# Rebuilding 64-bit weights with one pass on ScalarE instead of VectorE, and moving the softmax sums' chain one step

## The chip, the cores and the metric

The kernel runs on one core of a Trainium2 chip. Its time is device microseconds (us) of one execution; a median over runs is given. TensorE does the matmuls, VectorE and ScalarE the element work, GpSimd (POOL in the profile) the rest of it, and SyncE issues most of the DMAs. In the profile TensorE is PE (PEld is its weight load), VectorE is DVE, ScalarE is ACT and SyncE is SP.

## What is computed

Two batches of a three-stage block, in float32:

```
attention:  8 heads, 768 positions, head size 64
            scores = q k^T / 8; kept where key < n_sink (4) or 0 <= query - key < window (128)
            a = softmax(scores);  x = a v                        -> x: 2 x 768 x 512
MLP:        h = relu(x w_in)                      w_in 512 x 1024, given as 64-bit floats
            gate = sigmoid(conv over 3 positions of h)           conv_w 3 x 1024, 64-bit
            y = (h * gate) w_out                  w_out 1024 x 512, given as 64-bit floats
experts:    4 causal attention experts of size 64 on y, softmax, wo, weighted top-2 sum
```

## The kernel before

**Stages as steps.** The work is written out by hand as steps. `run_phases` (line 46) takes phases, each a start, a count and a list of stages with a lag, and emits at every step, in the order of the string `ORD1` (line 78), whatever stage is due then. Each engine runs its instructions in exactly that order. Attention of batch 0 (`a0`) takes steps 0 to 23: step i works on query tile qt = i // 4 (128 queries) and head pair pr = i % 4. Attention of batch 1 (`a1`) starts at step 24, the MLP (`m`) at step 30, the experts when both are through.

**Attention of batch 0 from qt = 2 on** (steps 8 to 23) is "overlaid" (`a1_S_overlaid`, line 506): TensorE writes the scores against the query tile's own keys into one PSUM bank (`own`) and those against the previous key tile into another (`old`); VectorE copies the old ones over the upper triangle of the own ones (line 518) and takes the maximum (line 519); ScalarE scales it (line 520) and takes the two exponentials with their sums (line 522). Every second step TensorE transposes four such tiles (line 571), ScalarE copies them out (line 574 through the helper at line 532), and GpSimd splits them with two selects (lines 575 and 577). GpSimd also copies the sink columns together (line 613).

**The sums' chain.** Once per query tile, after its last head pair, `attn_phase` (line 681) emits with a lag in steps taken from `LAGS[0]` (line 74): r (sum plus epsilon and reciprocal on VectorE, lines 527 and 528), rT (transpose on TensorE, line 545, copy, and a DMA store to DRAM, line 549), rB (two DMA loads that spread it over the partitions, line 556), xm (product with the attention output, line 560, VectorE, which frees the output's PSUM bank), xh (rounded copy, ScalarE, line 532), xl (the remainder, VectorE, line 670) and halo (small GpSimd copies). The order inside a step that matters here is: the weight background's first half (`more`), xl, S, sL, V, sV, xm, rT, sT, T, TT, the background's tail and second half (`misc`), r, xh.

**The weights.** Sixteen blocks of 128 x 512 64-bit numbers are loaded (line 379, two raw buffers; the load of block i+2 is issued after the last pass over block i) and each made into two float32r parts. `f64_fast` (line 334) makes the float from the upper word w1 and the lower word w0: mag (ScalarE, line 346, magnitude of w1, with an accumulated check), expo (VectorE, line 350, shift left by 3), top (VectorE, line 353, sign of w1), low (VectorE, line 356, three bits of w0). Then hi (line 538 or 540: ScalarE, VectorE or GpSimd by the letters of `WHI`) and lo (line 420, VectorE). mag of the next block is emitted together with low of this one.

**Their pace** is a budget of nominal nanoseconds (`background`, line 447): 550 a step in steps 4 to 23, 650 in 24 to 29, 1200 from step 30, each in two halves. A pass is emitted when its nominal cost (the list in `weight_steps`: 480 for expo, 860 for top, 860 for low) is in the budget. hi and lo are not in it: one of them is taken per step (`tail_step`), two from step 30.

The PSUM banks (8) are handed out to all of this by `psB` (line 117).

Of the kernel before, what the change touches and what calls it, by code (L numbers as in the profile page):

```python
# [12 lines left out]
U32 = mybir.dt.uint32  # L13
I64 = mybir.dt.int64
AF = mybir.ActivationFunctionType
ALU = mybir.AluOpType
# [8 lines left out]
KW = P + 2  # L25
# [14 lines left out]
F64_LO = 2.0**-15  # L40
F64_HI = 122879.9921875
GUARD = 2.0**-96
BIG = 3.0e38


# [25 lines left out]
BG0 = 550  # L71
BG1 = 650
BG2 = 1200
LAGS = ((1, 2, 1, 6, 4, 5, 6, 5, 2, 8, 8, 10, 11), (1, 1, 2, 6, 3, 4, 5, 3, 2, 5, 6, 7, 7))
LAGM = (1, 2, 3)
A2_N = 2
EVT = 'aaadadada'
# [11 lines left out]
class Kernel:  # L89
# [93 lines left out]
    def narrow(self):  # L183

        nc = self.nc
        g, ok = self.sm(1, "g"), self.guard
        nc.vector.tensor_scalar(ok, ok, GUARD, None, op0=ALU.is_lt)
        nc.vector.tensor_reduce(g, ok, axis=AX.X, op=ALU.add)
# [4 lines left out]
    def indices(self):  # L193
# [5 lines left out]
        nc.gpsimd.iota(self.kix, pattern=[[1, 2 * P]], base=0, channel_multiplier=0)  # L199
        nc.vector.tensor_scalar(z, rel[:, P:], 0.0, BIG, op0=ALU.is_lt, op1=ALU.mult)  # L200
        nc.vector.tensor_tensor(self.relx[:, P:], rel[:, P:], z, op=ALU.add)
# [132 lines left out]
    def f64_fast(self, raw, n, slot):  # L334

        nc = self.nc
        w = raw.bitcast(I32).rearrange("p (n two) -> p n two", two=2)  # L340
        w0, w1 = w[:, :, 0], w[:, :, 1]
        st = {}

        def mag():
            st["u"] = self.Wt([P, n], I32, "f64u")
            nc.scalar.activation(st["u"].bitcast(F32), w1.bitcast(F32), AF.Abs, scale=2.0**-111,
                                 accum_out=self.guard[:, slot : slot + 1])

        def expo():
            nc.vector.tensor_scalar(st["u"], st["u"], 3, None, op0=ALU.logical_shift_left)  # L350

        def top():
            nc.vector.scalar_tensor_tensor(st["u"], w1, -0x80000000, st["u"], op0=ALU.bitwise_and, op1=ALU.bitwise_or)

        def low():
            nc.vector.scalar_tensor_tensor(st["u"], w0, 29, st["u"], op0=ALU.logical_shift_right, op1=ALU.bitwise_or)
            st["c"] = st["u"].bitcast(F32)

        return st, [(0, mag), (480, expo), (860, top), (860, low)]

    def weight_steps(self):


        nc = self.nc
        order = []
        for f0 in range(0, NF, NF // 2):
            for f in range(f0, f0 + NF // 2 + 4):
                if f < f0 + NF // 2:
                    order.append((self.w_in, f, self.win))
                if f >= f0 + 4:  # L370
                    order.append((self.w_out, f - 4, self.wout))
        n = len(order)
        raws = {}

        def load(i):
            if i < n:
                src, f, _ = order[i]
                raws[i] = self.pRaw.tile([P, DM], I64, tag="raw", bufs=2, name=self.nm("raw"))
                nc.sync.dma_start(raws[i], src[f])

        boxes = [{} for _ in range(n)]

        def ahead(i):

            boxes[i]["st"], boxes[i]["ops"] = self.f64_fast(raws.pop(i), DM, i)
            boxes[i]["ops"][0][1]()

        steps = []
        if self.halves:
            steps.append((0, lambda: ahead(0)))  # L390
        for i in range(n):
            box = boxes[i]

            def step(i, k, box):
                if k == 0 and not self.halves:
                    box["st"], box["ops"] = self.f64_ops(raws.pop(i), DM)
                if k or not self.halves:
                    box["ops"][k][1]()
                if k == 3:
                    load(i + 2)  # L400
                    if self.halves and i + 1 < n:
                        ahead(i + 1)
                    self.tails.append([lambda: hi(i, box), lambda: lo(i, box)])

            steps += [(c, lambda i=i, k=k, box=box: step(i, k, box)) for k, c in enumerate((0, 480, 860, 860) if self.halves else (670, 335, 600, 600))]

        def part(i):
            _, f, dst = order[i]
            return [w[:, f].rearrange("p a c -> p (a c)") for w in dst]

        def hi(i, box):
            if self.halves:
                self.scaled(WHI[i], part(i)[0], box["st"]["c"], 2.0**-8)
            else:
                self.copy(WHI[i], part(i)[0], box["st"]["c"])

        def lo(i, box):
            h, l = part(i)
            if self.halves:
                nc.vector.scalar_tensor_tensor(l, box["st"]["c"], 2.0**-8, h.bitcast(F32), op0=ALU.mult, op1=ALU.subtract)  # L420
            else:
                nc.gpsimd.tensor_tensor(l, box["st"]["c"], h.bitcast(F32), op=ALU.subtract)
            self.ready.add((order[i][2][0].name, order[i][1]))

        return steps, lambda: (load(0), load(1))
# [30 lines left out]
    def a1_S(self, b, qt, pr):  # L456
# [39 lines left out]
        for j in range(2):  # L496
            nc.vector.tensor_tensor_reduce(out=Pt[:, j, :N], in0=ps[j][:, :N], in1=mask, scale=-SCALE,  # L497
                                           scalar=BIG, op0=ALU.add, op1=ALU.min, accum_out=nmx[:, j : j + 1])
        for j in range(2):
# [6 lines left out]
    def a1_S_overlaid(self, t, qt, pr, ps, Pt, nmx, sums):  # L506


        nc = self.nc
        w = KW + 2  # L510
        own, old = (x[:, : 2 * n].rearrange("p (j c) -> p j c", j=2) for x, n in zip(ps, (w, KW)))
        o = 2 * (qt % 2)
        for dst, kt in ((own[:, :, o : o + KW], qt), (old, qt - 1)):
            for j in range(2):
                nc.tensor.matmul(dst[:, j], t["q", qt][:, pr, j, :], t["k"][:, kt, pr, :], start=(j == 0), stop=(j == 1),
                                 skip_group_check=True)
        take = self.causal[:, 3 * P - o : 3 * P - o + KW].bitcast(I32)
        nc.vector.copy_predicated(own[:, :, 2 - o : 2 - o + KW], take[:, None, :].to_broadcast([P, 2, KW]), old)
        nc.vector.tensor_reduce(nmx, own, axis=AX.X, op=ALU.max, negate=True)
        nc.scalar.mul(nmx, nmx, SCALE)  # L520
        for j in range(2):
            nc.scalar.activation(Pt[:, j, :w], own[:, j], AF.Exp, bias=nmx[:, j : j + 1], scale=SCALE,
                                 accum_out=sums[:, j : j + 1])
# [225 lines left out]
    def attn_general(self, pool):  # L749
        nc = self.nc  # L750
        for b in range(B):
# [6 lines left out]
            for qt in range(NT):  # L758
# [10 lines left out]
                for h in range(H):  # L769
# [3 lines left out]
                    for c0, c1 in ((0, 4), (4, NT)):  # L773
# [5 lines left out]
                    nc.vector.tensor_tensor(pp, ps[:, :S], keep, op=ALU.mult)  # L779
                    nc.vector.tensor_tensor_reduce(out=pp, in0=pp, in1=pen, scale=-SCALE, scalar=BIG,  # L780
                                                   op0=ALU.add, op1=ALU.min, accum_out=nmx)
# [268 lines left out]
    def a2_S(self, b, qt, p, j):  # L1050
# [12 lines left out]
        for i, (lo, hi) in enumerate(pieces):  # L1063
# [6 lines left out]
            else:  # L1070
                nc.vector.tensor_tensor_reduce(out=Pt[:, lo:hi], in0=ps[:, : hi - lo], in1=self.causal[:, 4 * P + lo - hi : 4 * P], scale=-1.0,  # L1071
                                               scalar=BIG, op0=ALU.add, op1=ALU.min, accum_out=nm[:, i : i + 1])
        if len(pieces) == 2:
# [106 lines left out]
    def program(self, general):  # L1180
# [5 lines left out]
        with ExitStack() as ctx:  # L1186
# [34 lines left out]
            else:  # L1221
# [18 lines left out]
                self.fixed()  # L1240
                first = [self.attn_phase(b, b * NSTEP, LAGS[b], self.attn_misc(b)) for b in range(B)]
                m1 = NSTEP + MLP_START
# [109 lines left out]
```

## Time and profile before

| | |
|---|---|
| median of 3 runs | 380.1 us (378.39 to 380.71) |
| the profiled execution | 378.69 us |
| its span, first to last instruction | 377.0 us |
| TensorE clock granted | 0.996 |
| busy: PE / DVE / ACT / POOL | 359.7 / 275.9 / 259.9 / 132.0 us |

The profiled execution's span leaves 1.7 us of its time outside; the execution itself is 0.4% under the median. "Busy" of an engine is the time in which at least one of its instructions ran; where one instruction takes longer than its like, all of its duration counts. TensorE instructions overlap, and the modelled tail of a matmul can cover a short gap.

### The profile page before, as it was taken

What the parts mean: (1) busy time and instruction counts of PE and PEld (TensorE: products, weight loads), DVE (VectorE), ACT (ScalarE), POOL (GpSimd) and SP (SyncE); (2) the same over time, 40 slices, a digit from 0 to 9 for tenths busy, and PEclk for the clock granted to TensorE, in tenths of its full rate; (3) what the DMA queues carried; (4) which work ended last, traced back from release to release, by engine and by line L of the source; (5) the groups of instructions that cost most, each with busy time, mean ns of one, the idle gap of its engine ahead of it and who ended that gap; (6) DMA issues with size and microseconds to landing.
All of it is one profiled execution on the core that took longest, in us unless ns stands there. A gap on an engine that the chain in (4) does not pass through costs nothing.

```text
span 377.0 us, 8947 instructions
## 1 busy us (share of the span) xinstructions
PE 359.7 (95%) x3198; PEld 333.8 (89%) x3198; DVE 275.9 (73%) x800; ACT 259.9 (69%) x786; POOL 132.0 (35%) x254
## 2 busy tenths in 40 slices
PE   8898879999999999999999999999999999999994
PEld 5677767879899999999999999999999899978984
DVE  5589989889987997877865757237779697578631
ACT  4877768776876876635755875339878698859841
POOL 8016554244343333563521322310024134406310
PEclk9999999999999999999999999999999999999998
DMA  7953656433442301000111010000000010101112
GB/s 179 350 147 113 192 177 212 153 112 115 149 132 86 113 0 58 3 28 24 44 42 44 22 57 2 0 2 2 2 2 0 3 39 26 52 2 57 57 39 83
DMA packets 21844, 27.51 MB, mean 73 GB/s; under 512 B 2112, under 2 KB 14496, under 8 KB 21792
## 3 DMA queue, kind: packets, MB, share of 16 engines
q1 hardware_dynamic: 20560, 26.21, 21.9%
q10 hardware_dynamic: 1232, 0.66, 0.8%
q8 instruction: 27, 0.44, 0.5%
q14 instruction: 25, 0.20, 0.2%
HBM read 23.66 MB, written 3.19 MB: 71 GB/s over the span
## 4 chain that ended last, share of the span: by engine, by line
PE 65%; DVE 10%; ACT 6%; issue 2%; POOL 1%; DMA 1%; ACTq 0%; DVEq 0%
PE psB L854 15%; PE psB L810 14%; PE psB L1004 9%; PE psB L1128 5%; PE psB L932 5%; PE psB L1104 4%; PE psB L1152 3%; PE psB L640 2%; PE psB L1067 2%; PE psB L1066 2%; PE psB L483 2%; PE psB L598 1%; ACT P L1077 1%; ACT P L500 1%; DVE P L497 1%
## 5 line engine op out<-in xcount | busy, mean ns | idle before, releaser
L854 PE MATMUL psB<-g,wouthf 128*128 128x256 f32 x384 | 70.4, 281 | 0.3 <-POOL g L839 0.2
L854 PEld LDWEIGHTS psB<-g,wouthf 128*128 128x128 f32 x384 | 58.9, 188 | 0.7 <-POOL g L839 0.5
L1092 POOL TENSOR_SCALAR P<-P,r 128x256 f32<-128x256 f32 (+5 forms) x48 | 30.2, 643 | 82.5 <-DVE r L1090 45.6
L810 PE MATMUL psB<-xh,winhf 128*128 128x258 f32 x192 | 56.6, 295 | 0.0
L810 PE MATMUL psB<-xl,winhf 128*128 128x258 f32 x192 | 54.3, 283 | 0.0
L810 PE MATMUL psB<-xh,winlf 128*128 128x258 f32 x192 | 54.2, 282 | 0.0
L854 PE MATMUL psB<-g,woutlf 128*128 128x256 f32 x192 | 53.8, 280 | 0.0
L839 POOL TENSOR_TENSOR g<-ht,g 128x256 fp32r<-128x256 f32 x48 | 33.6, 701 | 52.9 <-ACT g L833 46.2
L826 ACT ACTIVATE ht<-ht 128x256 f32<-128x256 f32 x48 | 20.1, 419 | 27.9 <-DVE ht L824 27.8
L500 ACT ACTIVATE P<-P,nm 128x260 f32<-128x260 f32 (+2 forms) x64 | 30.5, 479 | 10.4 <-DVE nm L497 10.2
L831 DVE SCALAR_TENSOR_TENSOR ht<-ht 128x256 f32<-128x256 f32 x48 | 23.8, 496 | 18.7 <-ACT ht L826 18.7
L810 PEld LDWEIGHTS psB<-xh,winhf 128*128 128x128 f32 x192 | 36.4, 189 | 0.3 <-ACT ht L813 0.2
L810 PEld LDWEIGHTS psB<-xl,winhf 128*128 128x128 f32 x192 | 36.5, 190 | 0.0
L810 PEld LDWEIGHTS psB<-xh,winlf 128*128 128x128 f32 x192 | 36.3, 189 | 0.0
L854 PEld LDWEIGHTS psB<-g,woutlf 128*128 128x128 f32 x192 | 36.2, 188 | 0.0
L817 POOL TENSOR_SCALAR ht<-ht,cw 128x256 f32<-128x256 f32 x24 | 15.5, 648 | 56.9 <-ACT ht L813 51.4
L1077 ACT ACTIVATE P<-P,nm 128x256 f32<-128x256 f32 (+3 forms) x48 | 26.8, 561 | 4.7 <-DVE nm L1071 4.6
L824 DVE SCALAR_TENSOR_TENSOR ht<-ht,cw 128x256 f32<-128x256 f32 x48 | 27.7, 577 | 1.7
L1004 PE MATMUL psB<-yh,wqh 128*128 128x256 f32 x96 | 27.2, 283 | 0.0
L1004 PE MATMUL psB<-yl,wqh 128*128 128x256 f32 x96 | 27.0, 281 | 0.0
L1004 PE MATMUL psB<-yh,wql 128*128 128x256 f32 x96 | 26.9, 280 | 0.0
L1071 DVE CUSTOM_DVE_ANT_0 P<-psB,causal 128x256 f32<-128x256 f32 (+3 forms) x48 | 22.6, 485 | 5.8 <-PE psB L1067 5.4
(190 smaller groups left out, 1010.2 us busy)
## 6 DMA issues: line engine op xcount, KB each, us to landing
raw<-in_w_in_dram SPq DMA_DIRECT2D x8, 512.0 KB, 4.2
raw<-in_w_out_dram SPq DMA_DIRECT2D x8, 512.0 KB, 3.2
v<-in_v_dram SPq DMA_DIRECT2D x12, 256.0 KB, 5.2
R<-rD SPq DMA_DIRECT2D x24, 128.0 KB, 2.9
out_dram<-ot SPq DMA_DIRECT2D x11, 256.0 KB, 2.0
k<-in_k_dram SPq DMA_DIRECT2D x8, 260.0 KB, 3.9
raw<-in_wqkv_dram SPq DMA_DIRECT2D x8, 193.0 KB, 2.4
q<-in_q_dram SPq DMA_DIRECT2D x6, 256.0 KB, 3.2
```

Of the source, the lines that this page charges most:

```text
L500: nc.scalar.activation(Pt[:, j, :N], Pt[:, j, :N], AF.Exp, bias=nmx[:, j : j + 1], scale=-1.0, accum_out=sums[:, j : j + 1])
L810: nc.tensor.matmul(ps[:, :XW], w[:, f, kc, :], x[:, kc, :], start=(i == 0), stop=(i == len(ops) - 1))
L824: nc.vector.scalar_tensor_tensor(t1, h[:, 2 : 2 + CH], self.cw[:, 2 * NF + f : 2 * NF + f + 1], t1, op0=ALU.mult, op1=ALU.add)
L826: nc.scalar.activation(t1, t1, AF.Tanh)
L831: nc.vector.scalar_tensor_tensor(t1, t1, 1.0, h[:, 1 : 1 + CH], op0=ALU.add, op1=ALU.mult)
L839: eng.tensor_tensor(g[:, 1], t1, g[:, 0].bitcast(F32), op=ALU.subtract)
L854: nc.tensor.matmul(self.m1y[d // 2][:, d % 2, :], w[:, f, d, :], g[:, k], start=(first and i == 0 and d % 2 == 0), stop=(last and i == 2), ...
L932: nc.tensor.matmul(ps[:, :NVG], y[:, kc, ts_], w[:, kc, c0 : c0 + NVG], start=(i == 0), stop=(i == len(ops) - 1))
L1004: nc.tensor.matmul(ps, w[:, kc, c0 : c0 + P], y[:, kc, :], start=(i == 0), stop=(i == len(ops) - 1))
L1071: nc.vector.tensor_tensor_reduce(out=Pt[:, lo:hi], in0=ps[:, : hi - lo], in1=self.causal[:, 4 * P + lo - hi : 4 * P], scale=-1.0, scalar=B ...
L1077: nc.scalar.activation(Pt[:, lo:hi], src, AF.Exp, bias=nm[:, 0:1], scale=sg, accum_out=sums[:, j, i : i + 1])
L1092: nc.gpsimd.tensor_scalar(Ps[j][:, :N], Ps[j][:, :N], r[:, j : j + 1], 1.0, op0=ALU.mult, op1=ALU.mult)
```

## The change

Four edits. ScalarE gets one more pass per weight block (w0, read as an unsigned integer, is scaled and written back in place as its three upper bits); VectorE's three passes become two (shift u and join w0; then join the sign), and the third, `expo`, does nothing. The nominal cost of `expo` falls from 480 to 0. In `LAGS[0]` the entries r, rB, rT, xm, xh, xl and halo grow by one step. In the overlaid scores `old` takes the first bank and is computed first, `own` the second.

```diff
+LOW3 = (2.0**-29 * (1 - 2.0**-16), 7.5 * 2.0**-16 - 0.5)
...
-LAGS = ((1, 2, 1, 6, 4, 5, 6, 5, 2, 8, 8, 10, 11), (1, 1, 2, 6, 3, 4, 5, 3, 2, 5, 6, 7, 7))
+LAGS = ((2, 2, 1, 6, 4, 5, 6, 6, 3, 9, 9, 11, 12), (1, 1, 2, 6, 3, 4, 5, 3, 2, 5, 6, 7, 7))
...
             nc.scalar.activation(st["u"].bitcast(F32), w1.bitcast(F32), AF.Abs, scale=2.0**-111,
                                  accum_out=self.guard[:, slot : slot + 1])
+            nc.scalar.activation(w0, w0.bitcast(U32), AF.Copy, scale=LOW3[0], bias=LOW3[1])
 
         def expo():
-            nc.vector.tensor_scalar(st["u"], st["u"], 3, None, op0=ALU.logical_shift_left)
+            pass
 
         def top():
+            nc.vector.scalar_tensor_tensor(st["u"], st["u"], 3, w0, op0=ALU.logical_shift_left, op1=ALU.bitwise_or)
+
+        def low():
             nc.vector.scalar_tensor_tensor(st["u"], w1, -0x80000000, st["u"], op0=ALU.bitwise_and, op1=ALU.bitwise_or)
-
-        def low():
-            nc.vector.scalar_tensor_tensor(st["u"], w0, 29, st["u"], op0=ALU.logical_shift_right, op1=ALU.bitwise_or)
             st["c"] = st["u"].bitcast(F32)
 
-        return st, [(0, mag), (480, expo), (860, top), (860, low)]
+        return st, [(0, mag), (0, expo), (860, top), (860, low)]
...
-            steps += [(c, ...) for k, c in enumerate((0, 480, 860, 860) if self.halves else (670, 335, 600, 600))]
+            steps += [(c, ...) for k, c in enumerate((0, 0, 860, 860) if self.halves else (670, 335, 600, 600))]
...
-        own, old = (x[:, : 2 * n].rearrange("p (j c) -> p j c", j=2) for x, n in zip(ps, (w, KW)))
+        old, own = (x[:, : 2 * n].rearrange("p (j c) -> p j c", j=2) for x, n in zip(ps, (KW, w)))
-        for dst, kt in ((own[:, :, o : o + KW], qt), (old, qt - 1)):
+        for dst, kt in ((old, qt - 1), (own[:, :, o : o + KW], qt)):
```

## Rows read from the trace of the kernel before

**Rows 1.** The page's first part: busy time, share and instructions of each engine.
```profile
PE 359.7 (95%) x3198; PEld 333.8 (89%) x3198; DVE 275.9 (73%) x800; ACT 259.9 (69%) x786; POOL 132.0 (35%) x254
```

**Rows 2.** Windows: stretch, its length, busy us of each engine, granted clock, DMA.
```profile
18.67:54.45 35.78, 30.55 (x301) 26.71 (x303) 32.54 (x69) 25.50 (x105) 17.42 (x40) 1.00 0.51 159
65.00:111.00 46.00, 44.52 (x418) 40.30 (x418) 40.83 (x109) 33.60 (x101) 17.62 (x34) 1.00 0.40 130
```

**Rows 3.** Waits of PE, whole span: who for whom, us in total, times, longest.
```profile
PE psB L545 <- DVE su L528: 3.7, 5, 1.0
...
PE psB L515 <- DVE psB L518: 0.7, 1, 0.7
PE psB L640 <- ACT PT L532: 0.6, 1, 0.6
```

**Rows 4.** Timeline of DVE: start, duration, line; in brackets the idle time before.
```profile
43.07 0.42 DVE L518 COPY_PREDICATED psB<-causal,psB 128x260 f32<-128x260 int32 x1
43.53 0.43 DVE L519 TENSOR_REDUCE nm<-psB 128x2 f32<-128x264 f32 x1
43.88 0.68 DVE L560 TENSOR_TENSOR R<-psB,R 128x512 f32<-128x512 f32 x1
44.48 0.42 DVE L518 COPY_PREDICATED psB<-causal,psB 128x260 f32<-128x260 int32 x1
...
45.72 0.69 DVE L356 SCALAR_TENSOR_TENSOR f64u<-raw,f64u 128x512 int32<-128x512 int32 x1
46.33 0.61 DVE L527 TENSOR_SCALAR su<-su 128x8 f32<-128x8 f32 x1
46.97 0.20 DVE L528 RECIPROCAL su<-su 128x8 f32<-128x8 f32 x1
47.09 1.07 DVE L670 TENSOR_TENSOR xl<-R,xh 128x512 fp32r<-128x512 f32 x1
...
49.01 0.42 DVE L350 TENSOR_SCALAR f64u<-f64u 128x512 int32<-128x512 int32 x1
49.34 0.43 DVE L518 COPY_PREDICATED psB<-causal,psB 128x260 f32<-128x260 int32 x1
...
51.40 0.69 DVE L420 SCALAR_TENSOR_TENSOR winlf<-f64u,winhf 128x512 fp32r<-128x512 f32 x1 [0.85 <-ACT winhf L538]
52.01 1.12 DVE L353 SCALAR_TENSOR_TENSOR f64u<-raw,f64u 128x512 int32<-128x512 int32 x1
```

**Rows 5.** Timeline of POOL beside them.
```profile
45.76 1.15 POOL L575 TENSOR_SCALAR_AFFINE_SELECT PT<-PT 128x512 f32<-128x512 f32 x1 [1.58 <-ACT PT L532]
46.98 0.64 POOL L577 TENSOR_SCALAR_AFFINE_SELECT PT<-PT 128x512 f32<-128x512 f32 x1
...
51.61 0.98 POOL L577 TENSOR_SCALAR_AFFINE_SELECT PT<-PT 128x512 f32<-128x512 f32 x1
```

**Rows 6.** One source line each: durations min/median/max ns, first and last start.
```profile
L346 ACT ACTIVATE f64u<-raw x16: 653/670/698, 13.1 to 133.1; 128x512 f32<-128x512 f32 x16
...
L350 DVE TENSOR_SCALAR f64u<-f64u x17: 178/427/976, 10.8 to 137.0; 128x512 int32<-128x512 int32 x16, 128x24 int32<-128x24 int32 x1
...
L353 DVE SCALAR_TENSOR_TENSOR f64u<-raw,f64u x16: 673/684/1123, 15.0 to 140.3; 128x512 int32<-128x512 int32 x16
```

**Rows 7.** Timeline of ACT: mag, and the next maximum's scaling.
```profile
47.10 0.68 ACT L346 ACTIVATE f64u<-raw 128x512 f32<-128x512 f32 x1
...
49.12 0.20 ACT L520 ACTIVATE nm<-nm 128x2 f32<-128x2 f32 x1 [1.25 <-DVE nm L519]
```

**Rows 8.** Timeline of DVE, early MLP.
```profile
71.39 0.98 DVE L350 TENSOR_SCALAR f64u<-f64u 128x512 int32<-128x512 int32 x1 [1.54 <-ACT f64u L346]
```

**Rows 9.** Timeline of PE, early MLP.
```profile
76.60 0.71 PE L483 MATMUL psB<-k,q 64*128 64x130 f32 x6 [0.34 <-ACT PT L532]
77.81 0.27 PE L545 MATMUL psB<-ident,su 128*8 128x128 f32 x1 [0.50 <-DVE su L528]
```

**Rows 10.** DMA issues: KB each, us from issue to landing.
```profile
raw<-in_w_in_dram SPq DMA_DIRECT2D x8, 512.0 KB, 4.2
```

More of the change, by code (lines that the diff above doesn't have):

```diff
@@ L403, in step @@
                     self.tails.append([lambda: hi(i, box), lambda: lo(i, box)])
-            steps += [(c, lambda i=i, k=k, box=box: step(i, k, box)) for k, c in enumerate((0, 480, 860, 860) if self.halves else (670, 335, 600, 600))]
+            steps += [(c, lambda i=i, k=k, box=box: step(i, k, box)) for k, c in enumerate((0, 0, 860, 860) if self.halves else (670, 335, 600, 600))]
         def part(i):
```

## Prediction, made before the changed kernel ran

> **What bounds the kernel now.** I read the busy shares first, then windows, then the waits of TensorE, then the VectorE timeline. TensorE is busy for 359.7 of 377.0 us [rows 1], so most of the kernel can't become shorter by freeing another engine. The windows show where it can: in the 16 overlaid steps, 18.67 to 54.45 us, TensorE shows 30.55 of 35.78 us, VectorE 32.54, ScalarE 25.50 [rows 2]. TensorE's figure there is flattered: its waits in this stretch are mostly for the sums' reciprocal, 3.7 us in five waits over the whole span [rows 3]. The VectorE timeline shows passes nearly end to end, and its idle time is little, 35.78 - 32.54 = 3.2 us; the largest piece is 0.85 us for a rounded weight from ScalarE [rows 4]. So VectorE sets the pace of the overlaid steps, and each microsecond off its queue there is a microsecond off the end, as long as nothing else takes its place. In the early MLP, 65 to 111 us, TensorE has 44.52 of 46.00 [rows 2]: at most 1.5 us of visible idle is to be had. After 111 us VectorE doesn't hold TensorE up, and I cost the change there at nothing.
>
> Two things make VectorE's passes long. One is the work: from start to next start a weight pass takes 0.60 us (45.72 to 46.33), the shift of `expo` 0.33 (49.01 to 49.34), the product xm 0.60 (43.88 to 44.48), a score pair 0.81 (43.07 to 43.88) [rows 4]. The other is stretching: the 128 x 8 addition of r takes 0.61 us, the reciprocal of the same size behind it 0.20; xl takes 1.07 where the like passes take 0.68; `top` 1.12 where its median is 0.684 [rows 4, 6]. Each coincides with a GpSimd select: r ends just as the select of 45.76 to 46.91 does, xl overlaps the one from 46.98, `top` overlaps the one from 51.61, itself 0.98 instead of 0.64 [rows 5]. In the 16 steps I count r three times, xl three, `top` three and `expo` once so stretched (its longest is 0.976 against 0.427 [rows 6]; here I count 0.4): 3 x 0.41 + 3 x 0.39 + 3 x 0.44 + 0.4 = 4.1 us.
>
> **The change, part by part.**
>
> VectorE's weight work. A pass less per block is 16 x 0.33 = 5.3 us of VectorE in all. But the nominal cost of a block falls from 2200 to 1720, while the budget stays: blocks come every 3.1 steps instead of 4. Following the budget through steps 8 to 23: before 4 `expo`, 4 `top`, 4 `low`, 4 lo, 1 hi on VectorE; after 5, 6, 5 and 2, no `expo`. That is 4 more passes at 0.60, one hi at 0.33 more, 4 `expo` less: 2.4 + 0.33 - 1.32 = +1.4 us. xm's move takes one of four out of these steps: -0.6, so +0.8 there. In steps 24 to 29 the same count gives +0.2 for weights and +0.6 for the xm that arrives; TensorE is almost full by then, so I take half, +0.4. Sum **+1.2 us** of VectorE before the MLP: the saving is spent on an earlier finish. In steps 30 to 40 (65 to 111 us) the budget of 11 x 1200 pays for 7.7 blocks instead of 6.0; with 0.14 a block for hi that is 7.7 x 1.94 - 6.0 x 2.27 = +1.3 us on VectorE, 42 of 46 busy. TensorE's own work covers it (44.52 of 46.00). I take **+0.2**; without the cover it is +1.3. From step 41 on there is no weight work where there was some until 47, behind a full TensorE: 0.
>
> The sums' chain. r moves from the end of the step in which the selects run to the end of the next, where they are over, by the distance of 2.7 to 4.5 us between a score pair and its selects (43.07 against 45.76 to 47.62) [rows 4, 5]. Its stretch goes: **-1.2** (0 if the selects move too). xl moves from the step after the selects started to the one after that: **-0.8** of 1.2, between 0 and all. TensorE's wait for the reciprocal vanishes too; VectorE was busy during it, so 0. xm leaves the gap between two score pairs with little else between; then TensorE is late next: it waits for a bank from the earlier pair (0.7 us, once) [rows 3], and the attention output keeps its bank one step longer. I take **+0.2**, between 0 and 4 x 0.4 = 1.6. rT's store and rB's two loads move together, so their distance of three steps stays; on SyncE's queue they now stand behind the tile loads of the next step, which are needed four or more steps later: 0. halo and xh have five or more steps until the MLP needs them: 0.
>
> ScalarE's new pass. The trace has no such operation. The nearest row is mag, same strided input and size, 0.67 us [rows 6]; I take 0.58, mag's distance to the next instruction. That makes 16 x 0.58 = 9.3 us on ScalarE, 6 of them in steps 4 to 23, where it has 10.3 us of slack. By the Trainium skill's page "ScalarE: Activation LUTs", section "What ACT_TABLE_LOAD costs", an ACTIVATE with immediate scale and bias takes 186 ns plus 0.833 per element, an estimate of 613 ns here: 9.8 us in all by it instead of 9.3, with the path unchanged. Mag is followed by 1.25 us of waiting for the next maximum [rows 7], so the pass mostly fits; where it doesn't, it delays exponentials or a rounded weight. I take **+0.2**, between 0 and 14 x 0.58 = 8.1 if none of the 14 up to step 40 fits.
>
> What goes with `expo`. It came right behind mag, and VectorE waited for it; in the early MLP 1.54 us at one place [rows 8], after which TensorE lost 0.34 and 0.50 [rows 9]. `top` now follows a background step later: **-0.8**, bounds 0 and -1.5. Its own stretch in the overlaid steps: **-0.4**; a wait of 0.2 there: **-0.2**.
>
> Bank order of `own` and `old`: `old` is free after VectorE's copy, `own` after the exponentials; which wait shortens the trace doesn't tell: 0, between -0.7 and +0.7. Loads: a block lands in 4.2 us [rows 10]; blocks then come every 3.1 steps (7 us) and 1.4 steps (5.6 us): 0.
>
> Sum: 1.2 + 0.2 - 1.2 - 0.8 + 0.2 + 0.2 - 0.8 - 0.4 - 0.2 = **-1.6 us**. Against the profiled execution, 378.69, that is 377.1; this execution was 1.4 under the median of 380.1, so I forecast 380.1 - 1.6 = 378.5 for a median.
>
> **The rivals.**
>
> *The stretches stay.* If a pass collides wherever it is put, r and xl gain nothing, and 16 block passes of two SBUF inputs instead of 12 are exposed, a quarter of them stretched by 0.44: +2.0 + 0.4 on the forecast, 380.9. Rows 4 and 5 speak for it: three kinds of pass were hit. Against it: r, xl and `top` each met a select at a fixed place in the cycle, and the new pace of 3.1 steps breaks the cycle for the weights alone. The Trainium skill's page "SBUF — State Buffer", section "Who interferes with whom", states the rule this would follow: a VectorE instruction with two SBUF inputs, or in a two-port mode, and a GpSimd instruction reading SBUF exclude each other for a whole instruction. By that rule `top` and `low` contend as before, wherever they stand.
>
> *ScalarE becomes the bound* (slower). Place: the overlaid steps and steps 30 to 40. Per block it now runs 0.67 + 0.58 in one piece ahead of exponentials; blocks come more often. Price: from 0.2 up to 8.1 us; half exposed is +3.9, and the faster VectorE stretches then yield nothing (+2.0): 384.4. It decides once ScalarE no longer waits for the maximum (the 1.25 us of rows 7 gone). For it: a stall of TensorE on ScalarE's copy, 0.6 us [rows 3]. Against: 25.5 of 35.8 us busy, 6 passes add 3.5 and the two extra mags 1.5, to about 31.
>
> *All of it goes.* Every stretch (4.1) and the early MLP's idle (1.5) vanish, against +1.4 of work: 380.1 - 4.2 = 375.9. It needs `top` to miss the selects too.
>
> **How the numbers follow.** Forecast 0.50 (its own range 376.9 to 380), stretches stay 0.25, ScalarE bound 0.13, all goes 0.12. The range reaches from 375.6 to 382.8: it takes in all but the upper half of the ScalarE case, some of whose bound lies far above, and a tail below. One per cent is 3.8 us, about what a measurement of this kernel can tell from none. Faster by more (under 376.3): most of the last case and a tail of the forecast, 0.12. Slower by more (over 383.9): two thirds of the ScalarE case, 0.09. The rest, 0.79, is within 1%.
>
> **What would show it.** Line 350 gone, an ACT pass of 0.55 to 0.7 us sixteen times, the last sign pass near 110 us instead of 140.3 [rows 6]. The last overlaid step near 52.5 instead of 54.45. The addition of r at 0.2 us, the wait for it on TensorE gone; xl mostly at 0.7; the 1.54 us wait near 71 gone. Wrong it is if r or xl stay long, if the scaling of the maximum follows ScalarE's own work instead of VectorE, or if TensorE's waits for banks reappear in its waits by more than 1 us.

## The result: 1.35% slower, and the profile after

The changed kernel takes 384.37 us (median of 4 runs, 383.26 to 386.17) where the kernel before takes 379.75 (4 runs, 378.39 to 380.71): ratio 1.0135, interval [1.0103, 1.0167], some 4.6 us. The forecast was 378.5 and the range ended at 382.8, so the sign was wrong too. Of the rivals, "ScalarE becomes the bound" had 384.4. The profiled execution of the changed kernel took 383.26 us, its span is 381.5 (4.5 more than before), its granted clock 0.995 (0.996 before), so the clock is no part of the difference between these two executions.

Busy time on the page after; [rows 1] is its counterpart:

```profile
PE 360.1 (94%) x3198; PEld 333.5 (87%) x3198; DVE 268.7 (70%) x783; ACT 267.5 (70%) x803; POOL 132.5 (35%) x254
```

VectorE lost 7.2 us and 17 instructions, ScalarE gained 7.6 us and 17. TensorE does the same work; the span grew around it. Two windows of the changed kernel, the overlaid steps and steps 30 to 40 (columns as in [rows 2], and the same steps, not the same microseconds):

```profile
18.42:54.53 36.11, 29.96 (x301) 26.02 (x303) 30.85 (x69) 29.20 (x113) 16.40 (x40) 1.00 0.56 176
65.61:114.90 49.29, 45.73 (x422) 40.72 (x421) 43.61 (x110) 38.55 (x113) 21.03 (x35) 1.00 0.41 135
```

Steps 30 to 40 of the kernel before, which [rows 2] cuts at other places:

```profile
64.85:111.34 46.49, 45.01 (x423) 40.61 (x421) 41.17 (x111) 34.09 (x104) 17.62 (x34) 1.00 0.40 132
```

The overlaid steps take 36.11 us instead of 35.78, although VectorE does 1.7 us less. Steps 30 to 40 take 49.29 instead of 46.49, and there lie 2.8 of the 4.5 us. ScalarE has 3.7 us more in the first stretch and 4.5 in the second. By the start of the first MLP step (65.61 against 64.85) the changed kernel is 0.76 us late, by the end of step 40 3.56. After step 40 nothing more is lost: the last copy of an output tile, on ScalarE, comes 3.39 us later. Before and after:

```profile
372.04 0.37 ACT L532 COPY ot<-psB 128x256 f32<-128x256 f32 x1 [0.77 <-PE psB L1152]
```

```profile
375.43 0.37 ACT L534 COPY ot<-psB 128x256 f32<-128x256 f32 x1 [0.80 <-PE psB L1154]
```

From the end of this copy to the end of the span, with the last store of the output in it, there are 4.6 us before and 5.7 after. In the profiles of the experiments this end takes 4.2 to 5.5 us (4.3 with the weight change alone); with one profile of each kernel its 1.1 us can't be told from chance, and no step has a part in them. So the steps of the two traces have 3.4 us to explain.

VectorE in the changed kernel (start, duration, line, in brackets the idle time before):

```profile
43.37 1.12 DVE L355 SCALAR_TENSOR_TENSOR f64u<-f64u,raw 128x512 int32<-128x512 int32 x1
...
49.33 0.23 DVE L529 TENSOR_SCALAR su<-su 128x8 f32<-128x8 f32 x1
...
50.31 0.69 DVE L672 TENSOR_TENSOR xl<-R,xh 128x512 fp32r<-128x512 f32 x1
...
53.12 0.42 DVE L520 COPY_PREDICATED psB<-causal,psB 128x260 f32<-128x260 int32 x1
...
68.18 0.69 DVE L355 SCALAR_TENSOR_TENSOR f64u<-f64u,raw 128x512 int32<-128x512 int32 x1 [1.25 <-ACT raw L349]
...
70.69 0.68 DVE L358 SCALAR_TENSOR_TENSOR f64u<-raw,f64u 128x512 int32<-128x512 int32 x1
...
74.23 0.89 DVE L358 SCALAR_TENSOR_TENSOR f64u<-raw,f64u 128x512 int32<-128x512 int32 x1
```

r's addition takes 0.23 instead of 0.61 and xl 0.69 instead of 1.07 [rows 4]: the move did what was forecast to these two passes. Yet the last overlaid score pair starts at 53.12, where it started at 53.05 before. The pass that joins w0 still stretches to 1.12, and in the early MLP it now waits 1.25 us for ScalarE's new pass, which took the place of the 1.54 us of [rows 8].

The largest single stop, in full. ScalarE:

```profile
74.74 0.57 ACT L534 COPY PT<-psB 128x512 f32<-128x512 f32 x1
76.94 0.67 ACT L347 ACTIVATE f64u<-raw 128x512 f32<-128x512 f32 x1 [1.64 <-DMA raw<-in_w_in_dram]
77.52 0.19 ACT L347 ACTIVATION_READ_ACCUMULATOR f64u<-raw 128x1 f32 x1
77.61 0.65 ACT L349 ACTIVATE raw<-raw 128x512 int32<-128x512 uint32 x1
78.16 0.37 ACT L815 ACTIVATE ht<-psB 128x258 f32<-128x258 f32 x1
```

TensorE beside it:

```profile
76.19 0.29 PE L812 MATMUL psB<-xh,winlf 128*128 128x258 f32 x1
76.41 0.49 PE L485 MATMUL psB<-k,q 64*128 64x130 f32 x2
78.58 0.71 PE L485 MATMUL psB<-k,q 64*128 64x130 f32 x6 [1.69 <-ACT ht L815]
```

SyncE's issue of the load that ScalarE waits for:

```profile
72.41 0.36 SPq L381 DMA_DIRECT2D raw<-in_w_in_dram  x1
```

Read from the load: `low` at 70.69 ends at 71.37 and frees the raw buffer. SyncE issues the load at 72.41, 1.04 us later, behind other issues. The data is there at 76.86, by the chain of waits 4.45 us after the issue. But the next `low` came at 74.23, 3.5 us after the last, mag was emitted with it, and ScalarE was ready for mag at 75.30. It has one queue in order, so the relu of line 815, whose matmuls ended at 76.48, stands behind mag and the new pass until 78.16. The bank that it reads stays taken, and TensorE, which waits for the relu with its next scores, stops for 1.69 us. At [rows 9] scores of the same form lost 0.34.

TensorE's waits in the changed kernel (columns as in [rows 3]):

```profile
PE psB L547 <- DVE su L530: 2.4, 2, 1.3
PE psB L485 <- ACT ht L815: 2.3, 2, 1.7
...
PE psB L517 <- DVE psB L520: 0.8, 1, 0.8
```

The wait for the reciprocal fell from 3.7 to 2.4 and didn't vanish; the wait for ScalarE's relu is new. ScalarE's own waits, same columns:

```profile
ACT nm L522 <- DVE nm L521: 6.2, 7, 1.5
...
ACT f64u L347 <- DMA raw<-in_w_in_dram: 2.5, 2, 1.6
```

It waits 6.2 us for maxima where it waited 9.8 before, and 2.5 us for the loads of raw blocks: 1.64 at the stop above and 0.84 near 13 us, where the kernel before waits 0.38.

### The profile page after: what moved, and what is told of

Same layout as the page of the kernel before. It is cut to its first block, busy times and chain, and to the rows that moved or that the text cites. A ratio compares the mean times of both kernels' runs of the same rounds, so it can differ in the third digit from the quotient of the medians.

```text
span 381.5 us, 8970 instructions
## 1 busy us (share of the span) xinstructions
PE 360.1 (94%) x3198; PEld 333.5 (87%) x3198; DVE 268.7 (70%) x783; ACT 267.5 (70%) x803; POOL 132.5 (35%) x254
## 4 chain that ended last, share of the span: by engine, by line
PE 63%; ACT 10%; DVE 8%; issue 2%; POOL 1%; DMA 1%; ACTq 0%; DVEq 0%
PE psB L856 15%; PE psB L812 14%; PE psB L1006 9%; PE psB L1130 5%; PE psB L934 5%; PE psB L1106 4%; PE psB L1154 3%; ACT P L502 2%; PE psB L1069 2%; PE psB L485 2%; PE psB L1068 2%; PE psB L642 2%; ACT P L1079 1%; ACT f64u L347 1%; DMA raw<-in_w_in_dram 1%
```

## The experiments

The theory after the result: the change hurts through the **pace**. `expo` at a nominal cost of 0 makes a block cost 1720 instead of 2200 in the same budget, so mag and the new pass come more often than ScalarE, and the loads, can serve. Rivals: the new pass itself, the moved chain, or the order of the banks. Ratios are against the kernel before, run on the same chip, with their 95% interval.

**The weight change alone, with the old lags and bank order** (from the changed kernel)

```diff
-LAGS = ((2, 2, 1, 6, 4, 5, 6, 6, 3, 9, 9, 11, 12), ...)
+LAGS = ((1, 2, 1, 6, 4, 5, 6, 5, 2, 8, 8, 10, 11), ...)
...
-        old, own = (... zip(ps, (KW, w)))
+        own, old = (... zip(ps, (w, KW)))
...
```

> The changed kernel with the lags and the order of the two score banks as before: only the weights' passes and their pace are changed. Theory A (the weights' part alone costs it: ScalarE's second pass in one piece behind mag, and blocks that come every 1720 nominal ns instead of 2200): slower than before by 3.5 to 5.5 us, about as the whole change (+4.6). Theory B (the moved sums' chain or the banks cost it): within 1.5 us of before. If the moved chain brought the gain that I forecast (about 2 us), this one is slower than the changed kernel by 1 to 2 us.

Measured: 382.94 us, 1.0119 [1.0088, 1.0151]. The weight change carries the loss. Its last overlaid score pair starts at 53.33.

**The lags alone, in the kernel before**

```diff
-LAGS = ((1, 2, 1, 6, 4, 5, 6, 5, 2, 8, 8, 10, 11), ...)
+LAGS = ((2, 2, 1, 6, 4, 5, 6, 6, 3, 9, 9, 11, 12), ...)
```

> The kernel before with only the new lags (r, rT, rB, xm, xh, xl and halo a step later). Theory A: no slower than before; faster by 1 to 2 us if the stretched additions and remainders go (r from 0.61 to 0.2, xl from 1.07 to 0.7), 0 to -1 if something else takes their place. Theory B: slower by 2 to 4.6 us, with TensorE waiting for banks held one step longer.

Measured: 377.33 us, 0.9965 [0.9946, 0.9983]: -1.3 us. VectorE:

```profile
47.59 0.23 DVE L527 TENSOR_SCALAR su<-su 128x8 f32<-128x8 f32 x1
...
47.98 0.64 DVE L670 TENSOR_TENSOR xl<-R,xh 128x512 fp32r<-128x512 f32 x1
...
51.31 0.42 DVE L518 COPY_PREDICATED psB<-causal,psB 128x260 f32<-128x260 int32 x1
```

The same two passes are short, and here the last score pair does come earlier, 51.31 instead of 53.05. So the move is good by itself; in the changed kernel something else sets the steps.

**The whole change at the old pace**

```diff
-enumerate((0, 0, 860, 860) ...)
+enumerate((0, 480, 860, 860) ...)
```

> The changed kernel with the nominal cost of a block put back to 2200 (480 for the step that does nothing), so that blocks come at the pace of before; ScalarE's pass stays. Theory A1 (the pace is what costs: two more microseconds of ScalarE and VectorE per block in the same steps, raw loads that are late): 1 us slower to 2 us faster than before, ScalarE's wait of 1.64 us for a raw block gone. Theory A2 (the pass itself costs, wherever it stands): still 2.5 to 4 us slower than before.

Measured: 378.97 us, 1.0003 [0.9984, 1.0022]. One nominal cost, which emits no instruction, is worth 1.3% or 5.0 us. Steps 30 to 40 in this kernel:

```profile
63.60:111.02 47.42, 44.66 (x422) 40.29 (x420) 38.44 (x104) 37.60 (x110) 17.06 (x34) 1.00 0.43 139
```

They begin 1.25 us ahead of the kernel before, where the changed kernel is 0.76 late: in these traces the pace costs 2.0 us before the MLP. They take 47.42 us instead of 49.29: it costs another 1.9 there, and of the 2.8 us that these steps lost, 0.9 are lost at the old pace too. By the last copy of the output 3.3 us are left of the pace's cost.

**The new pace alone, with the three old VectorE passes**

```diff
-enumerate((0, 480, 860, 860) ...)
+enumerate((0, 480, 620, 620) ...)
```

> The kernel before, with its three VectorE passes and no new ScalarE pass, at the faster pace (nominal 480, 620 and 620, 1720 a block). Theory A1 (pace): slower than before by 2 us or more, and a wait of ScalarE for a raw block near 77 us. Theory A2 (ScalarE's pass): within 1.5 us of before.

Measured: 388.93 us, 1.0247 [1.0217, 1.0276]. The pace costs without the new pass, and more. So ScalarE's pass isn't what makes the pace bad, and VectorE's shorter work does relieve: at the same pace and with the old lags, the new passes lose 1.19% and the old ones 2.47%. Waits of ScalarE:

```profile
ACT f64u L346 <- DMA raw<-in_w_in_dram: 1.7, 2, 1.4
...
ACT f64u L346 <- DMA raw<-in_w_out_dram: 1.1, 1, 1.1
```

Here the clock takes a share that isn't separated: its runs had mean granted clocks of 0.981 to 0.990. At 0.981 it took 389.37 us, and the kernel with the weight change alone 385.72, one run each, so the new passes are the cheaper ones at an equal clock too. TensorE had been busy for 8.15 of the 10 us from 40 to 50 and 5.08 of the 6 us from 50 to 56, and the window after 56 us mixes the two levels of 1.2 and 2.4 GHz, 0.62 on average:

```profile
56.00:65.00 9.00, 7.47 (x48) 5.62 (x47) 6.82 (x27) 6.74 (x27) 4.55 (x12) 0.62 0.64 189
```

**The new pace only from the MLP on, or only before it** (from the changed kernel)

```diff
-BG0 = 550
-BG1 = 650
+BG0 = 430
+BG1 = 508
```

```diff
-BG2 = 1200
+BG2 = 938
```

> The changed kernel with the budgets of steps 4 to 29 cut by 1720/2200 (430 and 508), so that blocks come at the old pace there and at the new one (1.43 steps a block) only from step 30. If the new pace costs in the MLP steps (ScalarE and VectorE are given 28% more weight work per step there, raw loads late): slower than before by 2 to 4 us, as the changed kernel's loss from step 30 to 41 (2.8 us). If it costs in the attention steps, where the changed kernel reaches the first MLP step 0.76 us later and the kernel at the old pace 1.25 us earlier: within 1 us of before.

> The changed kernel with the MLP's budget cut by the same factor (1200 to 938): new pace in the attention steps, old pace from step 30. If the new pace costs in the MLP steps: first MLP step 0.76 us late as in the changed kernel, and hardly more lost after it, 0 to 1.5 us slower than before in all. If it costs in the attention steps and the rest only follows: 3 us or more slower.

Measured: 381.48 us, 1.0068 [1.0045, 1.0091] with the pace in the MLP alone; 382.72, 1.0087 [1.0063, 1.0111] in attention alone. Both stretches pay, and their sum, 1.55%, is about the whole 1.35% within the intervals. The clock doesn't explain the second: a run at a granted clock of 1.000 took 382.19 us. ScalarE's waits for w_in's raw blocks in the first:

```profile
ACT f64u L347 <- DMA raw<-in_w_in_dram: 3.2, 3, 1.4
```

and in the second, where blocks come slowly in the MLP:

```profile
ACT f64u L347 <- DMA raw<-in_w_in_dram: 1.0, 1, 1.0
```

In each, one wait of 1.0 to 1.1 us stands near 13 us, as in the changed kernel at the old pace; from step 30 on ScalarE waits 2.1 us in the first and not at all in the second.

**Without the loads of raw blocks 2 to 15** (the changed kernel works on the first two blocks again and again, at the same pace, and leaves these loads out)

```diff
...
+                if i >= 2 and self.halves:
+                    raws[i] = kept[i % 2]
+                    return
...
```

> The changed kernel at its new pace, with the loads of the raw blocks 2 to 15 left out: the blocks are made from the first two over and over, so the weights are wrong, and nothing else is left out. If the late raw loads are what makes the new pace dear (ScalarE waits 1.64 us at 76.94, its queue behind it): at least 2 us faster than the changed kernel, 381.5 or less. If it is the element work itself: within 1 us of the changed kernel.

Measured: 381.33 us, 1.0057 [1.0036, 1.0078]. Between the medians that is 3.0 us of the 4.6, by the two intervals 1.5 to 4.4; between runs at the same granted clock of 0.995 it is 1.6 to 1.9 (383.26 against 381.32 and 381.65). Both what ScalarE waits for and the traffic are gone, so the figure holds both; and 0.57% are lost without these loads. In the trace the gain lies in steps 30 to 40, 48.01 us instead of 49.29:

```profile
65.93:113.94 48.01, 46.14 (x423) 40.86 (x421) 42.81 (x110) 38.73 (x113) 19.87 (x35) 1.00 0.20 61
```

The same place as the stop above (lines stand 3 further from line 383 on):

```profile
75.04 0.58 ACT L537 COPY PT<-psB 128x512 f32<-128x512 f32 x1
75.51 0.69 ACT L347 ACTIVATE f64u<-raw 128x512 f32<-128x512 f32 x1
...
76.17 0.68 ACT L349 ACTIVATE raw<-raw 128x512 int32<-128x512 uint32 x1
76.73 0.41 ACT L818 ACTIVATE ht<-psB 128x258 f32<-128x258 f32 x1
```

TensorE beside it:

```profile
76.72 1.17 PE L488 MATMUL psB<-k,q 64*128 64x130 f32 x8
```

Mag follows the copy without a gap, the relu comes 1.4 us earlier, and the scores start with no wait.

**Old pace, and the new pass apart from mag** (in the slot of `expo`, a background step later)

```diff
-            nc.scalar.activation(w0, w0.bitcast(U32), AF.Copy, scale=LOW3[0], bias=LOW3[1])
 
         def expo():
-            pass
+            nc.scalar.activation(w0, w0.bitcast(U32), AF.Copy, scale=LOW3[0], bias=LOW3[1])
...
-enumerate((0, 0, 860, 860) ...)
+enumerate((0, 480, 860, 860) ...)
```

> The kernel at the old pace and with the new lags, ScalarE's new pass no longer right behind mag but half a step or more later, in the slot (480) of the step that did nothing. If 1.2 us of ScalarE in one piece is what delays exponentials and copies: 1 to 2 us faster than before. If only the sum of ScalarE's work counts: as the kernel at the old pace, within 0.7 us of before.

Measured: 378.01 us, 0.9969 [0.9951, 0.9986]; the changed kernel at the old pace had 1.0003, and the two intervals just touch. ScalarE does an xh copy, a maximum and two exponentials between mag and the pass (lines from 350 on stand one earlier):

```profile
37.03 0.69 ACT L347 ACTIVATE f64u<-raw 128x512 f32<-128x512 f32 x1
37.61 0.20 ACT L347 ACTIVATION_READ_ACCUMULATOR f64u<-raw 128x1 f32 x1
37.70 0.62 ACT L533 CAST xh<-R 128x512 fp32r<-128x512 f32 x1
...
39.63 0.71 ACT L351 ACTIVATE raw<-raw 128x512 int32<-128x512 uint32 x1
```

The last overlaid score pair starts 1.5 us earlier than in the changed kernel at the old pace (52.05):

```profile
50.51 0.42 DVE L519 COPY_PREDICATED psB<-causal,psB 128x260 f32<-128x260 int32 x1
```

The last copies of the output are 1.6 us apart in the two traces, the same way. So what ScalarE does in one piece counts, as the ScalarE rival had it.

**The same with the old order of the banks** (`own` first)

```diff
-        old, own = (... zip(ps, (KW, w)))
+        own, old = (... zip(ps, (w, KW)))
...
```

> The kernel at the old pace with the pass apart (378.0 us, 0.9969 of before), with the order of the two score banks as before: own first, old second. If the order of the banks does nothing, as I had it in the prediction: ratio to before 0.995 to 0.999. If it is what the gain of that kernel rests on: 1.000 or above.

Measured: 377.82 us, 0.9971 [0.9952, 0.9989]. The order of the banks is worth nothing that shows, in this version.

**Three more roundings moved from ScalarE to VectorE** (old pace, pass apart; blocks 10, 11 and 15)

```diff
-WHI = 'aadaddapdpaaddda'
+WHI = 'aadaddapdpdddddd'
```

> The kernel at the old pace with the pass apart, with the rounded copies of the weight blocks 10, 11 and 15 on VectorE instead of ScalarE. That kernel reaches MLP step 34 4.2 us earlier than the one before and keeps 1.5 us of it at step 46. If ScalarE's load in the MLP steps takes the rest back: 3 x 0.54 us less there give 0.5 to 1.5 us more gain, ratio 0.993 to 0.996. If not ScalarE but VectorE or the loads take it back: 0.997 or above.

Measured: 376.30 us, 0.9916 [0.9897, 0.9935]. It beats both kernels. Part of the 0.84% is the clock: its six runs were granted 0.996 to 1.000, and the kernel before, at 0.996 or more on the same chip, took 378.2 to 379.1 us, so at an equal clock some 0.5% are left. Steps 30 to 40 with the pass apart, and with the roundings moved too:

```profile
62.06:109.46 47.40, 45.00 (x422) 40.28 (x421) 38.63 (x106) 37.49 (x109) 17.23 (x34) 1.00 0.42 139
```

```profile
61.92:108.60 46.68, 44.77 (x423) 40.30 (x421) 38.83 (x104) 36.63 (x107) 17.64 (x35) 1.00 0.42 137
```

ScalarE is busy 0.9 us less, and these steps are 0.7 us shorter. That fits the aim of the edit: VectorE's freed time goes to work that ScalarE is late with.

**A still slower pace in attention** (from the version with the pass apart)

```diff
-BG0 = 550
-BG1 = 650
+BG0 = 484
+BG1 = 572
```

> The kernel at the old pace with the pass apart, with the budgets of steps 4 to 29 cut by another 12% (484 and 572): 0.8 of a block less before the MLP, which keeps 1200. If weight work costs in the attention steps one for one (0.8 x 2 us of VectorE) and the MLP hides it: ratio 0.991 to 0.995. If the MLP steps are as full: 0.996 to 1.000.

Measured: 377.70 us, 0.9946 [0.9923, 0.9969], not apart from the 0.9969 of 550 and 650. Its runs fall apart by the clock: three at 0.996 or more took 375.9 to 376.4 us, three at 0.990 and 0.991 took 379.2 to 379.3. The kernel of the bank experiment above, with 550 and 650, took 377.3 to 378.5 at 0.996 or more on the same chip, so at an equal clock the slower pace does gain. The trace is of a run at 0.991. In it the steps of the MLP start 4.5 to 6.2 us ahead of the kernel before until step 46 (by the first matmul of each step), 0.5 ahead at step 50 and 0.5 behind at step 55. On the way TensorE stops for a weight that isn't ready, and then runs slowly; its stop, and the window behind it:

```profile
146.87 0.50 PE L855 MATMUL psB<-g,wouthf 128*128 128x256 f32 x2 [1.65 <-ACT wouthf L539]
```

```profile
149.00:155.00 6.00, 6.00 (x32) 5.57 (x31) 4.43 (x14) 3.02 (x8) 0.00 (x0) 0.50 0.00 0
```

The granted clock of these 6 us is 0.50, the level of 1.2 GHz; it was 1.00 up to 148 us, with TensorE idle for 1.9 of the 3 us from 145 on. At half the clock 6 us hold 3 us of work, so stop and clock together are an estimated 4.9 us, about the whole loss between steps 46 and 55.

**Both: the roundings moved, and the slower pace in attention**

```diff
-BG0 = 550
-BG1 = 650
+BG0 = 484
+BG1 = 572
...
-WHI = 'aadaddapdpaaddda'
+WHI = 'aadaddapdpdddddd'
```

> The two changes that helped, together: old pace, pass apart, three rounded copies on VectorE, and the slower budget of steps 4 to 29. If what they relieve is separate (ScalarE in the MLP steps, VectorE in the attention steps): ratio to before 0.988 to 0.991. If the attention steps' gain is only handed to full MLP steps: as with the copies alone, 0.990 to 0.993, or worse.

Measured: 376.47 us, 0.9922 [0.9892, 0.9953]: by the median no better than moving the roundings alone. Again the clock decides: three runs at 0.997 and 0.998 took 375.1 to 376.0 us (the roundings alone, at 0.996 to 1.000, 375.9 to 376.8), two at 0.991 took 378.1 and 378.2, and the trace, of one of these two, shows a granted clock of 0.53 from 149 to 155 us behind the same wait for a weight.

A third raw buffer, with each load issued a block earlier, would test the loads without leaving them out. It wasn't tried.

## Why the prediction was wrong, point by point

The measured 1.35% splits along the experiments, each step one edit or one group of edits: lags -0.35%, the new passes at the old pace +0.38% (1.0003 - 0.9965), the new pace +1.32% (1.0135 - 1.0003).

- **The sums' chain** (-1.2 for r, -0.8 for xl, +0.2 for xm: -1.8): right. The passes have the durations that were forecast, and alone the move gives -1.3 us, interval -2.0 to -0.6. At the new pace it gives nothing that shows (1.0135 with it and the bank order, 1.0119 without): as the ScalarE rival said, "the faster VectorE stretches then yield nothing".
- **Bank order** (0): right, as far as tested (at the old pace, with the pass apart).
- **Everything on the weights** came to +0.2 in the sum (1.2 + 0.2 + 0.2 - 0.8 - 0.4 - 0.2) and measured +4.5 us. Three steps failed: the loads put at nothing, the cover of ScalarE's new pass, and the faster blocks counted in VectorE's time alone, in the MLP and before it.
- **"Loads: a block lands in 4.2 us [rows 10]; blocks then come every 3.1 steps (7 us) and 1.4 steps (5.6 us): 0"** is a term put at nothing that wasn't: leaving the loads out gains 3.0 us between the medians (1.5 to 4.4) and 1.3 in steps 30 to 40 of the traces. The landing time was right (4.5 for w_in and 3.9 for w_out after), the lead was not. 5.6 us is the mean distance of blocks. What counts is the shortest distance between two `low` passes, 3.5 us at 70.69 and 74.23, because the budget releases whole passes twice a step; and from the lead goes SyncE's queue, 1.04 us. 1.04 + 4.45 = 5.5 us were needed from the end of one `low`, and ScalarE asked after 3.9.
- **"ScalarE's new pass ... +0.2"**. Its size was nearly right, 0.664 us each, 0.55 to the next instruction against 0.58 taken. Its cover was not: mean slack of an in-order queue didn't cover a piece of 1.2 us. Setting the pass apart from mag gives back about a third of a per cent at the old pace. The sign I had named for this case, the waits for the maximum gone, was too crude: they only fell from 9.8 to 6.2 us, and to 6.1 at the old pace, where nothing is lost.
- **The early MLP** (+0.2, and -0.8 for `expo`'s waits): measured +2.8 us in steps 30 to 40: 0.9 that the old pace has too, and 1.9 from the pace, of which 1.3 go with the loads. VectorE's more work there was put at 1.3 and was 2.4 (43.61 against 41.17); whether TensorE's work covered it, as I assumed, no run separates. ScalarE's and the loads', from the same faster blocks, weren't priced there. The wait that went with `expo` came back as the wait for the new pass; that TensorE's two losses of [rows 9], some 5 us after that wait, came of it, no row shows.
- **Weight work before the MLP** (+1.2): right that the saving is spent on an earlier finish, but counted in VectorE's time alone. At the first MLP step the pace costs 2.0 us (0.76 late against 1.25 early at the old pace), in the traces more than the loads cost. How much of this is the piece of 1.2 us and how much other waits, no run separates.
- **The stretches of the weight passes** (-0.4 with `expo`): the joins still stretch to 1.12 and 1.13 us. That rival was right for them alone.

The last sign pass, now the last pass over a block, starts at 116.8, not near 110; before, the last pass started at 141.0. So the weights were ready some 24 us earlier, and TensorE's waits in the kernel before show none for a weight. That is the error in one line: I followed the budget through the steps for VectorE, found the saving spent, and stopped there, where the faster blocks go on to ScalarE, SyncE and the loads.

The ScalarE rival came within 0.1 us of the result. Its place (overlaid steps and steps 30 to 40) and the fate of VectorE's gain were right, its mechanism half: the pass matters by blocking the queue, but a good part of the price is the pace's late loads, of which it said nothing. That its number came so near is in part luck. The new pace without the new pass is worse still.

## What to carry to other kernels

When a pass of a background job gets cheaper, its nominal cost is not bookkeeping: lowering it speeds up everything else that a block needs, on the other engines, the queues and the loads. Check each of them at the shortest distance between two blocks, not at the mean. Take the saving as slack first, and spend it on work from the engine that is late: here the old pace, the pass set apart and three moved roundings turned 1.0135 into 0.9916.

## What the runs showed of the hardware

A strided in-place ACTIVATE from uint32 to int32 takes more than a plain estimate gives:

```profile
L349 ACT ACTIVATE raw<-raw x16: 648/664/727, 13.6 to 109.4; 128x512 int32<-128x512 uint32 x16
```

The median is 664 ns; the estimate of 613 from the Trainium skill's page "ScalarE: Activation LUTs", section "What ACT_TABLE_LOAD costs", is 51 ns short. That changes no conclusion.

A VectorE pass can lose more to GpSimd than the 0.44 us used in the prediction. In the changed kernel, VectorE:

```profile
30.30 1.71 DVE L422 SCALAR_TENSOR_TENSOR winlf<-f64u,winhf 128x512 fp32r<-128x512 f32 x1 [1.06 <-ACT winhf L540]
```

GpSimd beside it:

```profile
30.19 1.28 POOL L303 TENSOR_TENSOR vsr<-vs,vsr 128x512 fp32r<-128x512 f32 x1
```

The pass takes 1.71 us instead of 0.69, and ends 0.54 us after GpSimd's instruction, near the 0.60 that a weight pass needs from start to next start. The rule weighed in the prediction (the Trainium skill's page "SBUF — State Buffer", section "Who interferes with whom": two SBUF inputs on VectorE and a GpSimd instruction that reads SBUF exclude each other for a whole instruction) agrees with that. In the overlaid steps r and xl escaped, as the move took them away from the selects; later, at 76.08, r's addition takes 0.70 us, beside a GpSimd instruction from 75.47 to 76.75.
